# Column halves for the second batch's products with v, later scores, and dummy products only in idle steps

## Chip, cores and metric

The kernel runs on one core of a Trainium2 chip, in one launch. The metric is the device time of that core in microseconds; lower is better. Its engines are named as in the profile: PE (TensorE, with its weight loads as PEld), DVE (VectorE), ACT (ScalarE), POOL (GpSimd) and SP, which issues the DMAs.

## What is computed

Two batches of 12480 tokens of width 128. Per batch, 49 agents attend to all keys and gather v; then every query attends to the 49 agents; the result goes through a layer of width 2048 with a rational activation.

```python
def sm(a, b):
    s = scale * (a @ b.transpose(0, 2, 1))
    s = s - s.max(-1, keepdims=True)
    e = np.exp(s)
    return e / (e.sum(-1, keepdims=True) + 1e-09)
a2k = sm(agents, k)
agent_v = a2k @ v
q2a = sm(q, agents)
x = q2a @ agent_v                       # reshaped to (24960, 128)
h = x @ w_in
P = a[0] + a[1] * h + a[2] * h**2 + a[3] * h**3
Q = 1.0 + np.abs(b[0]) * np.abs(h) + np.abs(b[1]) * h**2
out = (P / (Q + 1e-06)) @ w_out
```

## The kernel before

All is float32. The first batch's attention over its keys (scores, maximum, exponentials, products with v) runs ahead of the loop, some 60 us. Its result, 49 x 128, is folded with `w_in` into a matrix of 49 rows and 2048 columns per batch (`m_pe`, L275, rounded to a high part `m_hi` and a rest `m_lo` in `m_rnd` and `m_rest`), so that the hidden layer of a block of 480 tokens is the product of this matrix with the transposed query weights `pT`.

The loop in `main` goes over 278 units of three chunks (128 hidden columns by 480 tokens). Sixteen chunks make a block of tokens; batch two begins in unit 138. Step `i` issues, each engine in its own order:

- ACT (`act`): the square of unit i (L501, out of the PSUM slot `slots[i % 2]` into `x`), and in turn the logarithm (L515) or the exponential (L517) of two earlier units.
- DVE: `dve2(i)` (L530) and `dve1(i)` (L522), which read the same slot; for one unit in four also the last product (L535).
- POOL: the last product of unit i-6 (L568) for the other three in four, and L573.
- PE: `mm1(i+1)` (L439, L440: six products into the other slot), in the first seven steps two dummy products (L578) into `outs[0]`, from step 7 on `mm2(i-7)` (L447: three products, two passes each in the trace, summed in `outs[0]` or `outs[1]`), and then one piece of attention work into the other bank of `outs`.

That piece comes from `attend`. It asks three streams in turn: `q_stream` (the queries of later blocks: scores L374, L379, L380, exponentials, transposes L401 with copies L406), `w_stream` (decoding the rest of `w_out`, L175 to L185, in the first steps), and `a2k_stream` (the second batch's attention over its keys). Each stream gives at most one item in a step. An item may hold one piece of PE work, and only one such piece goes into a step: who comes later in the list waits. What an item asks of ACT, DVE and POOL is put into `hold` and runs in the next step, behind that step's own work on the engine.

`a2k_stream` works in groups of four chunks of 128 keys (`G1 = 4`; 98 chunks are 24 groups of four and one of two): two empty items, then 25 items with scores (`sc_pe`, L222; copy by ACT, L640; maximum by DVE in `group_max`, L200 and L203), the maximum over partitions (`mx_pe1`, `mx_pe2`), 25 items with products with v (`pv_pe`, L253: each chunk's exponentials, 128 x 49, as weights, its v, 128 x 129, as the moving side, summed over the group in rows 0 to 48 of a bank; DVE adds the bank to `av_acc`, L257 and L259), the division (`av_norm`), a transpose, and four `m_pe`. In one step of ten (`K_REST`) this stream rests. All of it has to be done before unit 138.

A score group writes the bank that the group before it filled, so its first product waits until DVE's L200 has read that bank.

Of the kernel before, what the change touches and what calls it, by code (L numbers as in the profile page):

```python
# [11 lines left out]
F32 = mybir.dt.float32  # L12
# [4 lines left out]
ALU = mybir.AluOpType  # L17
# [4 lines left out]
C = 128  # L22
A = 49
DFF = 2048
NFC = DFF // 128
# [4 lines left out]
NCK = -(-N // CK)  # L30
NKP = NCK * CK
KR = 113
LO = 64
BT = 480
# [22 lines left out]
OUT_DVE = range(40, 50)  # L57

K_REST = 10
NUT, NWT, NXT = 9, 4, 2  # L60
KB, VB = 6, 6

# [8 lines left out]
WARM, DUM, DUA = 8, 2, 4  # L71
# [9 lines left out]
def agent_attention_rational_moe(  # L81
# [12 lines left out]
    PE, ACT, DVE, POOL, SP = nc.tensor, nc.scalar, nc.vector, nc.gpsimd, nc.sync  # L94

    const = ctx.enter_context(tc.tile_pool(name="const", bufs=1))
# [7 lines left out]
    ident = const.tile([128, 128], F32, name="ident")  # L104
# [12 lines left out]
    mb = const.tile([CK, 2, A], F32, name="mb")  # L117
    m49 = const.tile([A, 2], F32, name="m49")
    av_acc = const.tile([A, C + 1], F32, name="av_acc")
    avt = const.tile([128, KR], F32, name="avt")  # L120
    m_hi = [const.tile([128, DFF], F32R, name=f"m_hi{b}") for b in range(B)]
    m_lo = [const.tile([128, DFF], F32R, name=f"m_lo{b}") for b in range(B)]
# [126 lines left out]
    def pv_pe(b, G, g, bank, first, last):  # L249
        vt = v_t.pop((b, g))  # L250
        n = min(G, NCK - g * G)
        for c in range(n):
            PE.matmul(bank[:A, :C + 1], lhsT=S[:, g * G + c, :], rhs=vt[:, c, :], start=first and c == 0, stop=last and c == n - 1)  # L253

    def pv_ev(first, bank):
        if first:
            DVE.tensor_copy(out=av_acc, in_=bank[:A, :C + 1])  # L257
        else:
            DVE.tensor_tensor(out=av_acc, in0=bank[:A, :C + 1], in1=av_acc, op=ALU.add)  # L259

    def av_norm(src):
        r = ring(sm_p, 1, [A, 1], F32, "avr")
        DVE.tensor_scalar(out=r, in0=src[:, C:C + 1], scalar1=EPS, scalar2=None, op0=ALU.add)
        DVE.reciprocal(out=r, in_=r)
        DVE.tensor_scalar(out=av_acc[:, :C], in0=src[:, :C], scalar1=r, scalar2=co["rho_s"][:A], op0=ALU.mult, op1=ALU.mult)
# [150 lines left out]
    def main(wk, streams, fast):  # L416
# [54 lines left out]
        def attend(bank, blk, switching, i):  # L471
            used = switching
            for s in range(len(streams)):
                if s == 2 and i % K_REST == K_REST - 1:
                    break
                while True:
                    if nxt[s] is None:
                        nxt[s] = next(streams[s], "end")
                    if nxt[s] == "end":
                        break  # L480
                    need, pe, evs = nxt[s]
                    if need is not None:
                        if need > blk // 2 + 1:
                            break
                        nxt[s] = None
                        continue
                    if pe is not None:
                        if used:
                            break
                        used = True  # L490
                        pe(bank)
                    for e, f in evs:
                        hold[e].append(lambda f=f: f(bank))
                    nxt[s] = None
                    break

        def act(i):
            if i < NU:
# [52 lines left out]
        for i in range(NU + lag):  # L551
            act(i)
            run_hold("ACT")
            g = i - gap
            fin = [g] if 0 <= g < NU and not on_pool(g) else []
            if i == NU - 1:
                dve_last(fin.pop())
            if i < NU:
                dve2(i)
                dve1(i)  # L560
            for u in fin:
                dve_last(u)
            run_hold("DVE")
            if done is not None:
                out_ev(done)
                done = None
            if 0 <= g < NU and on_pool(g):
                POOL.tensor_tensor(out=view("u", g), in0=view("u", g), in1=view("w", g), op=ALU.mult)  # L568
            run_hold("POOL")
            a = (i, i, -1, i - 1)[i % ON_DVE]  # L570
            if 0 <= a < NU and on_pool(a):
                y = view("u", a)
                POOL.tensor_scalar(out=y, in0=y, scalar1=1.0, scalar2=arm["om"], op0=ALU.mult, op1=ALU.add)  # L573
            if i + 1 < NU:
                mm1(i + 1)
            if i < lag:
                for _ in range(DUM):
                    PE.matmul(outs[0][:, :BT], lhsT=wo[:, 0, :], rhs=wi[:, :BT], start=True, stop=True)  # L578
            cur = 0
            if i >= lag:  # L580
                done = mm2(i - lag)
                cur = units[i - lag][-1] // NFC
            if i > 0:
                attend(outs[1 - cur % 2], units[min(i + 1, NU - 1)][-1] // NFC, done is not None, i)
        if done is not None:
            out_ev(done)

# [38 lines left out]
    def a2k_stream(kv, b, G):  # L626
        ng = -(-NCK // G)
        load_k(kv, b, G, 0, 2)
        load_k(kv, b, G, 1, 2)
        yield (None, None, [])  # L630
        yield (None, None, [])
        for g in range(ng):
            if 1 <= g < ng - 1:
                load_k(kv, b, G, g + 1, 2)
            if g >= ng - 2:
                load_v(kv, b, G, g + 2 - ng, 2)

            def cp(bk, g=g):
                n = min(G, NCK - g * G)
                ACT.copy(out=S[:, g * G:g * G + n, :], in_=bk[:CK, :n * A].rearrange("p (c a) -> p c a", a=A))  # L640

            yield (None, lambda bk: sc_pe(b, G, g, bk), [("ACT", cp), ("DVE", lambda bk, g=g: group_max(G, g, bk))])
        row = 3 * ((ng - 2) // 2 % 2 == 0)
        yield (None, lambda bk: mx_pe1(bk, mx[:, row, :]), [("DVE", lambda bk: mx_ev1(bk))])
        yield (None, lambda bk: mx_pe2(bk), [("DVE", lambda bk: mx_ev2(bk))])
        for g in range(-2, ng):
            evs = []
            if g + 2 < ng:
                evs.append(("POOL", lambda bk, g=g: ex_sub(G, g + 2, POOL)))
            if 0 <= g + 1 < ng:  # L650
                evs.append(("ACT", lambda bk, g=g: ex_exp(G, g + 1)))
            if g < 0:
                yield (None, None, evs)
                continue
            if 1 <= g < ng - 1:
                load_v(kv, b, G, g + 1, 2)
            evs.append(("DVE", lambda bk, g=g: pv_ev(g == 0, bk)))
            yield (None, lambda bk: pv_pe(b, G, g, bk, True, True), evs)
        yield (None, None, [("DVE", lambda bk: av_norm(av_acc))])
        yield (None, avt_pe, [("DVE", avt_ev)])  # L660
        for pc in range(4):
            yield (None, lambda bk: m_pe(pc, bk), [("ACT", lambda bk: m_rnd(b, pc, bk)), ("DVE", lambda bk: m_rest(b, pc, bk))])
# [191 lines left out]
```

## Time and profile before

| | |
|---|---|
| median of three runs | 1321.06 us (1320.81 to 1327.85) |
| the profiled execution's own time | 1321.58 us |
| its span, first to last instruction | 1319.7 us |
| busy PE, DVE, ACT, POOL | 95%, 91%, 88%, 87% |
| mean granted PE clock | 0.992 |

Four engines are busy at once nearly all the time, so the busy shares alone name no bound. The steps are to be read stage by stage: the first steps of the loop (about 68 to 116 us), the steps with the second batch's scores (to about 313 us), those with its products with v (345 to 585 us), and the steps after 640 us, which hold only query work. PE's records overlap: a product's duration includes its way through the array, so what a product costs PE is read from one start to the next.

### The profile page before, as it was taken

How to read it: one execution, taken by the hardware profiler on the slowest of the kernel's cores; microseconds unless marked ns; L12 is line 12 of the kernel's file. 1: busy time of each engine (PE TensorE's matmuls, PEld its weight loads, DVE VectorE, ACT ScalarE, POOL GpSimd, SP SyncE). 2: the span in 40 equal slices, each digit the busy share in tenths (PEclk: the TensorE clock that was granted, in tenths of full speed). 3: DMA queues.
4: the chain of work that ended last, by engine and by line, in shares of the span. 5: the costliest groups of instructions: out<-in, count | busy, mean ns of one | idle time of the engine just before them, and what ended most of it. 6: DMA issues, size and time to landing. Idle time of an engine off the chain costs nothing.

```text
span 1319.7 us, 13309 instructions
## 1 busy us (share of the span) xinstructions
PE 1255.2 (95%) x4815; PEld 786.3 (60%) x4815; DVE 1196.1 (91%) x984; ACT 1166.5 (88%) x736; POOL 1153.7 (87%) x562
## 2 busy tenths in 40 slices
PE   8979999998999999998999999999999999999998
PEld 8756666665566566665555555655655555565553
DVE  5888999989988888988999999999999999999996
ACT  3468999998889898997999999999999999999995
POOL 3448988988999998988899999999999999999991
PEclk9989999999999999999999999999999999999999
DMA  9411111111011111100000000000000000000000
GB/s 367 184 48 47 40 55 46 40 59 38 22 57 47 41 53 48 39 27 23 16 23 30 23 15 23 23 15 23 30 23 15 23 23 31 8 30 8 16 7 26
DMA packets 22971, 56.55 MB, mean 43 GB/s; under 512 B 2800, under 2 KB 9712, under 8 KB 22896
## 3 DMA queue, kind: packets, MB, share of 16 engines
q1 hardware_dynamic: 22896, 55.61, 12.7%
q8 instruction: 40, 0.66, 0.2%
q14 instruction: 35, 0.29, 0.1%
HBM read 42.82 MB, written 12.78 MB: 42 GB/s over the span
## 4 chain that ended last, share of the span: by engine, by line
PE 47%; DVE 23%; ACT 13%; POOL 9%; issue 6%; DMA 1%; SPq 0%; DVEq 0%; POOLq 0%; ACTq 0%
PE outb L447 25%; DVE u L522 8%; DVE w L530 8%; PE slot L439 8%; PE slot L440 7%; ACT x L501 6%; POOL u L568 5%; ACT w L517 3%; POOL u L573 3%; PE outb L374 3%; ACT w L515 2%; DVE u L535 2%; PE outb L253 2%; PE bank L209 1%; PE outb L222 1%
## 5 line engine op out<-in xcount | busy, mean ns | idle before, releaser
L447 PE MATMUL outb<-u,wo 128*128 128x480 f32 x1664 | 726.2, 571 | 36.6 <-DVE pT L406 21.4
L568 POOL TENSOR_TENSOR u<-u,w 128x1440 f32<-128x1440 f32 x204 | 668.6, 3290 | 0.0
L530 DVE SCALAR_TENSOR_TENSOR w<-slot,cf,x 128x1440 f32<-128x1440 f32 x278 | 474.9, 1708 | 89.8 <-ACT x L501 85.0
L447 PEld LDWEIGHTS outb<-u,wo 128*128 128x128 f32 x1664 | 309.5, 189 | 314.3 <-issue 230.5
L501 ACT ACTIVATE x<-slot,cf 128x1440 f32<-128x1440 f32 x278 | 405.5, 1459 | 96.7 <-PE slot L440 68.4
L522 DVE SCALAR_TENSOR_TENSOR u<-x,cf,slot 128x1440 f32<-128x1440 f32 x278 | 472.6, 1700 | 0.0
L573 POOL TENSOR_SCALAR u<-u,cf 128x1440 f32<-128x1440 f32 x204 | 387.8, 1902 | 93.7 <-DVE u L522 72.5
L439 PE MATMUL slot<-pT,m_hi 113*128 113x480 f32 x832 | 375.6, 452 | 10.9 <-DVE u L522 10.5
L515 ACT ACTIVATE w<-w,cf 128x2880 f32<-128x2880 f32 (+1 forms) x140 | 374.6, 2676 | 0.0
L517 ACT ACTIVATE w<-w 128x2880 f32<-128x2880 f32 (+1 forms) x140 | 361.8, 2585 | 0.0
L440 PE MATMUL slot<-pT,m_lo 113*128 113x480 f32 x832 | 317.4, 382 | 0.0
L439 PEld LDWEIGHTS slot<-pT,m_hi 113*128 113x128 f32 x832 | 157.6, 189 | 82.8 <-DVE u L522 40.9
L440 PEld LDWEIGHTS slot<-pT,m_lo 113*128 113x128 f32 x832 | 157.9, 190 | 40.8 <-issue 23.4
L535 DVE SCALAR_TENSOR_TENSOR u<-u,cf,w 128x1440 f32<-128x1440 f32 x74 | 134.0, 1816 | 0.0
L374 PEld LDWEIGHTS outb<-ag,q 128*120 128x120 f32 x400 | 45.6, 185 | 12.7 <-issue 8.2
L374 PE MATMUL outb<-ag,q 128*120 128x49 f32 x400 | 44.9, 265 | 0.9 <-DVE pT L406 0.7
L401 PEld LDWEIGHTS outb<-ident,p 120*113 120x113 f32 x200 | 27.5, 177 | 23.2 <-issue 20.0
L222 PEld LDWEIGHTS outb<-ag,k 128*128 128x128 f32 x196 | 26.4, 197 | 15.7 <-issue 8.8
L406 DVE CAST pT<-outb 113x480 fp32r<-113x480 f32 x50 | 32.4, 648 | 0.0
L454 ACT COPY o<-outb 128x480 f32<-128x480 f32 x42 | 23.0, 547 | 9.2 <-PE outb L447 9.2
L253 PEld LDWEIGHTS outb<-v,S 128*49 128x49 f32 x196 | 20.3, 123 | 17.6 <-issue 12.0
L401 PE MATMUL outb<-ident,p 120*113 120x120 f32 x200 | 29.2, 267 | 0.0
(132 smaller groups left out, 504.3 us busy)
## 6 DMA issues: line engine op xcount, KB each, us to landing
q<-qT SPq DMA_DIRECT2D x26, 480.0 KB, 3.4
outT<-o SPq DMA_DIRECT2D x52, 240.0 KB, 2.0
v<-vP SPq DMA_DIRECT2D x24, 258.0 KB, 2.7
k<-kT SPq DMA_DIRECT2D x24, 256.0 KB, 2.6
v<-vP SPq DMA_DIRECT2D x9, 645.0 KB, 11.1
k<-kT SPq DMA_DIRECT2D x8, 640.0 KB, 8.9
raw<-w_in SPq DMA_DIRECT2D x4, 512.0 KB, 10.8
raw<-w_out SPq DMA_DIRECT2D x2, 512.0 KB, 10.6
```

The costliest lines, as they stand in the source:

```text
L374: PE.matmul(bank[:CH, c * A:(c + 1) * A], lhsT=qt[:, c * CH:(c + 1) * CH], rhs=ag[:, b * A:(b + 1) * A], start=True, stop=True)
L439: PE.matmul(s[:, j, :BT], lhsT=m_hi[b][:KR, f], rhs=rhs, start=True, stop=False)
L440: PE.matmul(s[:, j, :BT], lhsT=m_lo[b][:KR, f], rhs=rhs, start=False, stop=True)
L447: PE.matmul(outs[blk % 2][:, :BT], lhsT=wo[:, fc, :], rhs=g[:, j, :], start=fc == 0, stop=fc == NFC - 1)
L501: ACT.activation(out=x, in_=h, func=AF.Square, bias=co["xb"])
L515: ACT.activation(out=r, in_=r, func=AF.Ln, bias=arm["lb"])
L517: ACT.activation(out=r, in_=r, func=AF.Exp, scale=-1.0)
L522: DVE.scalar_tensor_tensor(out=y, in0=x, scalar=co["kap"], in1=h, op0=ALU.add, op1=ALU.mult)
L530: DVE.scalar_tensor_tensor(out=w, in0=h, scalar=co["mu"], in1=x, op0=ALU.max, op1=ALU.add)
L535: DVE.scalar_tensor_tensor(out=view("u", u), in0=view("u", u), scalar=arm["om"], in1=view("w", u), op0=ALU.add, op1=ALU.mult)
L568: POOL.tensor_tensor(out=view("u", g), in0=view("u", g), in1=view("w", g), op=ALU.mult)
L573: POOL.tensor_scalar(out=y, in0=y, scalar1=1.0, scalar2=arm["om"], op0=ALU.mult, op1=ALU.add)
```

## The change

Three edits. `K_WAIT = 6` puts six empty items ahead of the scores in place of two. The dummy products move behind `attend` and are issued only where `attend` issued no PE work in the step (`attend` now returns `used`). The products with v of the second batch (`pv2_pe`) put even chunks of a group into rows 0 to 48 of the bank and odd chunks into rows 64 to 112, each half with its own start and stop; DVE adds 113 rows instead of 49 to a new tile `av_two` (`pv2_ev`), and at the end one product with the identity brings the upper half down (`pv2_sum`) and DVE adds the halves (`pv2_both`), ahead of `av_norm` in the item that held only that.

```diff
+K_WAIT = 6
+    av_two = const.tile([KR, C + 1], F32, name="av_two")
...
+    def pv2_pe(b, G, g, bank):
+        vt = v_t.pop((b, g))
+        n = min(G, NCK - g * G)
+        for c in range(n):
+            o = c % 2 * LO
+            PE.matmul(bank[o:o + A, :C + 1], lhsT=S[:, g * G + c, :], rhs=vt[:, c, :], start=c < 2, stop=c >= n - 2)
...
+    def pv2_ev(first, bank):
         if first:
-            DVE.tensor_copy(out=av_acc, in_=bank[:A, :C + 1])
+            DVE.tensor_copy(out=av_two, in_=bank[:KR, :C + 1])
         else:
-            DVE.tensor_tensor(out=av_acc, in0=bank[:A, :C + 1], in1=av_acc, op=ALU.add)
+            DVE.tensor_tensor(out=av_two, in0=bank[:KR, :C + 1], in1=av_two, op=ALU.add)
+
+    def pv2_sum(bank):
+        PE.matmul(bank[:A, :C + 1], lhsT=ident[LO:KR, LO:KR], rhs=av_two[LO:KR, :], start=True, stop=True)
+
+    def pv2_both(bank):
+        DVE.tensor_tensor(out=av_acc, in0=bank[:A, :C + 1], in1=av_two[:A, :], op=ALU.add)
+        av_norm(av_acc)
...
-            if i < lag:
-                for _ in range(DUM):
-                    PE.matmul(outs[0][:, :BT], lhsT=wo[:, 0, :], rhs=wi[:, :BT], start=True, stop=True)
...
-            if i > 0:
-                attend(outs[1 - cur % 2], units[min(i + 1, NU - 1)][-1] // NFC, done is not None, i)
+            used = i > 0 and attend(outs[1 - cur % 2], units[min(i + 1, NU - 1)][-1] // NFC, done is not None, i)
+            if i < lag and not used:
+                for _ in range(DUM):
+                    PE.matmul(outs[0][:, :BT], lhsT=wo[:, 0, :], rhs=wi[:, :BT], start=True, stop=True)
...
-        yield (None, None, [])
-        yield (None, None, [])
+        for _ in range(K_WAIT):
+            yield (None, None, [])
...
-            evs.append(("DVE", lambda bk, g=g: pv_ev(g == 0, bk)))
-            yield (None, lambda bk: pv_pe(b, G, g, bk, True, True), evs)
-        yield (None, None, [("DVE", lambda bk: av_norm(av_acc))])
+            evs.append(("DVE", lambda bk, g=g: pv2_ev(g == 0, bk)))
+            yield (None, lambda bk: pv2_pe(b, G, g, bk), evs)
+        yield (None, pv2_sum, [("DVE", pv2_both)])
```

Counted over the order of PE's work, this moves as follows. Before, score groups stand in steps 3, 4, 5, 6 and then 10 to 51, the products with v in steps 61 to 110, the last `m_pe` in step 121. Now the first score group stands in step 10 (in steps 7 to 9 the query stream holds the place or the key stream rests), the last in 57, the products with v in 66 to 117, `pv2_sum` in 120, the last `m_pe` in step 130.

Two places in the order. First PE in steps 4 and 5, before (`k1` is a group of keys, `ag` the agents, `outb` a bank of `outs`; L439 and L440 are `mm1`, L578 the dummies, L222 a score group):

```order
L578 MATMUL outb0_67<-wi_78,wo_79 128x480 x2
L222 MATMUL outb1_68<-ag_71,k1_1_647 128x49 x4
L439 MATMUL slot0_605<-pT_0_566,m_hi0_86 128x480
L440 MATMUL slot0_605<-pT_0_566,m_lo0_88 128x480
...
L578 MATMUL outb0_67<-wi_78,wo_79 128x480 x2
L222 MATMUL outb1_68<-ag_71,k1_0_645 128x49 x4
```

and now (L457 and L458 are `mm1`, L602 the dummies):

```order
L602 MATMUL outb0_67<-wi_78,wo_79 128x480 x2
L457 MATMUL slot0_606<-pT_0_567,m_hi0_87 128x480
L458 MATMUL slot0_606<-pT_0_567,m_lo0_89 128x480
...
L602 MATMUL outb0_67<-wi_78,wo_79 128x480 x2
L457 MATMUL slot1_607<-pT_0_567,m_hi0_87 128x480
```

The scores are gone from between the dummies and the next `mm1`; in step 1 it is the dummies that are gone, ahead of the query scores.

Second DVE in steps 4 to 6, before (`w`, `u`, `x`: the loop's tiles; `qs`: the query sums, L387 and L388; `wo`: the decoded weights, L185; `mx`: the scores' maximum):

```order
L522 SCALAR_TENSOR_TENSOR u_4_632<-x_0_641,cf_74,slot0_605 128x1440
L387 TENSOR_REDUCE qs_1_755<-e1_91 120x8
L388 RECIPROCAL qs_1_755<-qs_1_755 120x8
L185 SCALAR_TENSOR_TENSOR wo_79<-u_6_634 128x512
L200 TENSOR_REDUCE mx_81<-outb1_68 128x49
L530 SCALAR_TENSOR_TENSOR w_2_639<-slot1_606,cf_74,x_1_642 128x1440
L522 SCALAR_TENSOR_TENSOR u_5_633<-x_1_642,cf_74,slot1_606 128x1440
L185 SCALAR_TENSOR_TENSOR wo_79<-w_3_640 128x512
L200 TENSOR_REDUCE mx_81<-outb1_68 128x49
L530 SCALAR_TENSOR_TENSOR w_3_640<-slot0_605,cf_74,x_0_641 128x1440
```

and now (L549 and L541 are `dve2` and `dve1`):

```order
L541 SCALAR_TENSOR_TENSOR u_4_633<-x_0_642,cf_74,slot0_606 128x1440
L405 TENSOR_REDUCE qs_1_749<-e1_92 120x8
L406 RECIPROCAL qs_1_749<-qs_1_749 120x8
L188 SCALAR_TENSOR_TENSOR wo_79<-u_6_635 128x512
L549 SCALAR_TENSOR_TENSOR w_2_640<-slot1_607,cf_74,x_1_643 128x1440
L541 SCALAR_TENSOR_TENSOR u_5_634<-x_1_643,cf_74,slot1_607 128x1440
L188 SCALAR_TENSOR_TENSOR wo_79<-w_3_641 128x512
L549 SCALAR_TENSOR_TENSOR w_3_641<-slot0_606,cf_74,x_0_642 128x1440
```

The maxima of the scores have left the first steps; nothing else changed its place there.

## Rows read from the trace of the kernel before

**Rows 1.** The page: the chain that ended last, shares of the span by engine.

```profile
PE 47%; DVE 23%; ACT 13%; POOL 9%; issue 6%; DMA 1%; SPq 0%; DVEq 0%; POOLq 0%; ACTq 0%
```

**Rows 2.** Windows: stretch, length, busy PE, PEld, DVE, ACT, POOL; clock, DMA share, GB/s.

```profile
115.99:312.73 196.74, 190.65 (x775) 124.70 (x776) 179.12 (x153) 179.66 (x120) 176.07 (x78) 1.00 0.16 48
374.67:599.56 224.89, 218.53 (x852) 134.66 (x852) 199.43 (x162) 204.66 (x132) 207.39 (x108) 1.00 0.14 42
753.38:1138.11 384.73, 368.13 (x1290) 221.36 (x1288) 362.99 (x258) 364.10 (x204) 365.79 (x161) 1.00 0.07 23
```

**Rows 3.** The same stretches, line L530 alone, which has one instruction a step.

```profile
115.99:312.73 196.74, 73.70 (x43) 1.00 0.16 48
374.67:599.56 224.89, 82.23 (x48) 1.00 0.14 42
753.38:1138.11 384.73, 153.96 (x90) 1.00 0.07 23
```

**Rows 4.** The chain of waits from 374 to 600 us: shares by line, one piece.

```profile
by line: PE outb L447 39.6%; PE slot L439 13.0%; PE slot L440 11.2%; PE outb L253 8.4%; DVE w L530 5.3%; ACT x L501 4.5%; DVE u L522 4.3%; PE outb L374 2.9%; DVE u L535 2.6%; issue 2.4%; ACT w L517 1.2%; ACT w L515 1.1%; DVE av_acc L265 1.1
...
404.15 2.42 PE outb L447 x6
```

**Rows 5.** Timeline of PE and PEld around one group of products with v (start, us).

```profile
353.34 1.77 PE L447 MATMUL outb<-u,wo 128*128 128x480 f32 x4
355.04 0.83 PEld L253 LDWEIGHTS outb<-v,S 128*49 128x49 f32 x8 [0.70 <-issue]
355.05 1.09 PE L253 MATMUL outb<-v,S 128*49 128x129 f32 x8
356.06 0.48 PE L439 MATMUL slot<-pT,m_hi 113*128 113x480 f32 x1
356.39 0.38 PE L440 MATMUL slot<-pT,m_lo 113*128 113x480 f32 x1
356.60 0.38 PE L439 MATMUL slot<-pT,m_hi 113*128 113x480 f32 x1
```

**Rows 6.** Groups by line: these products' durations (min/median/max ns), and two copies by DVE.

```profile
L253 PE MATMUL outb<-v,S x196: 271/273/313, 355.0 to 584.1; 128*49 128x129 f32 x196
...
L238 DVE COPY mb<-outb 128x49 f32<-128x49 f32 x3 | 0.6, 204 | 0.9 <-PE outb L235 0.9
...
L257 DVE COPY av_acc<-outb 49x129 f32<-49x129 f32 x1 | 0.3, 278 | 0.0
```

**Rows 7.** Timeline of PE in steps 3 to 5, two score groups among them.

```profile
82.36 0.99 PE L222 MATMUL outb<-ag,k 128*128 128x49 f32 x8
84.53 0.49 PE L439 MATMUL slot<-pT,m_hi 113*128 113x480 f32 x1 [1.19 <-DVE u L522]
...
85.95 1.77 PE L578 MATMUL outb<-wi,wo 128*128 128x480 f32 x4
91.42 1.88 PE L222 MATMUL outb<-ag,k 128*128 128x49 f32 x8 [3.70 <-DVE mx L200]
93.09 0.75 PE L439 MATMUL slot<-pT,m_hi 113*128 113x480 f32 x1
```

**Rows 8.** Window behind PE's idle stretch (columns as Rows 2).

```profile
91.50:98.30 6.80, 6.80 (x18) 4.99 (x19) 4.86 (x5) 2.87 (x4) 5.62 (x6) 0.50 0.14 39
```

**Rows 9.** Waits from 86 to 120 us (total us, times, longest).

```profile
DVE w L530 <- ACT x L501: 3.6, 3, 1.9
```

**Rows 10.** Timeline of DVE and POOL from step 4 to step 10.

```profile
87.88 1.70 DVE L522 SCALAR_TENSOR_TENSOR u<-x,cf,slot 128x1440 f32<-128x1440 f32 x1
...
97.42 3.29 POOL L568 TENSOR_TENSOR u<-u,w 128x1440 f32<-128x1440 f32 x1
...
110.18 1.46 POOL L573 TENSOR_SCALAR u<-u,cf 128x1440 f32<-128x1440 f32 x1
114.06 2.79 POOL L573 TENSOR_SCALAR u<-u,cf 128x1440 f32<-128x1440 f32 x1 [2.42 <-DVE u L522]
116.82 3.28 POOL L568 TENSOR_TENSOR u<-u,w 128x1440 f32<-128x1440 f32 x1
```

More of the change, by code (lines that the diff above doesn't have):

```diff
@@ L253, in pv_pe @@
             PE.matmul(bank[:A, :C + 1], lhsT=S[:, g * G + c, :], rhs=vt[:, c, :], start=first and c == 0, stop=last and c == n - 1)
-    def pv_ev(first, bank):
+    def pv2_pe(b, G, g, bank):
[5 more added lines that the diff above has]
+    def pv2_ev(first, bank):
         if first:
-            DVE.tensor_copy(out=av_acc, in_=bank[:A, :C + 1])
+            DVE.tensor_copy(out=av_two, in_=bank[:KR, :C + 1])
         else:
-            DVE.tensor_tensor(out=av_acc, in0=bank[:A, :C + 1], in1=av_acc, op=ALU.add)
+            DVE.tensor_tensor(out=av_two, in0=bank[:KR, :C + 1], in1=av_two, op=ALU.add)
[4 more added lines that the diff above has]
+        av_norm(av_acc)
     def av_norm(src):
@@ L495, in attend @@
                     break
+            return used
         def act(i):
```

## The prediction

> **What bounds the kernel now.** The chain that ended last runs 47% through PE, 23% through DVE, 13% through ACT [rows 1]: no engine holds the whole time, so I went from the page to windows over stages. Three stretches with an even mix of steps, each cut at the start of a step, give the busy time of every engine [rows 2], and the same stretches with L530 alone give the number of steps [rows 3]. A step takes 196.74 / 43 = 4.575 us while the second batch's scores run, 224.89 / 48 = 4.685 us while its products with v run, and 384.73 / 90 = 4.275 us with neither. PE is busy 97% of the first two stretches and the others 89 to 92% [rows 2]; in the products' stretch the chain is 75% PE (L447, L439, L440, L253, L374) [rows 4]. So PE leads there, with the others close behind.
>
> From this come two prices on the path. The first stretch holds 21 score groups (counted in the order), each with ACT's copy and DVE's maximum: (4.575 - 4.275) x 43 / 21 = 0.61 us a group. The second holds 22 groups of products with v: (4.685 - 4.275) x 48 / 22 = 0.89 us. PE's own time for one of these is more: a pass of `mm2` takes 2.42 / 6 = 0.40 [rows 4], so the four from 353.34 would end their turn at 354.94; the group starts at 355.05, L439 at 356.06, and L440 comes 0.33 later, where the next pass takes 0.21 or 0.22. That is 0.11 + 1.01 + 0.11 = 1.23 us [rows 5]. So 0.89 / 1.23 = 0.73 of PE's time shows in the end.
>
> The loop's first steps are another matter. DVE paces them; but in step 4 PE's queue stops for 3.70 us at a score group that needs the bank which L200 has yet to read, until 91.42 [rows 7]. Behind it stands `mm1(6)`, whose slot was free when L522 of step 4 ended at 89.58 [rows 10]. It starts at 93.09, at half clock: PE did nothing for those 3.70 us, and the granted clock is 0.50 (1.2 GHz) from 91.5 to 98.3 [rows 8]. DVE then waits three times for ACT's squares, 3.6 us in all [rows 9].
>
> **The change, part by part.** *Scores out of steps 3 to 6.* PE's queue then holds only `mm1` and dummies, and `mm1(6)` can start at about 89.6, 3.5 us earlier. DVE's 3.6 us of waits go, and four maxima with them. What is late next is POOL. Its first L568, at 97.42, hangs on decoded weights that DVE delivers hardly sooner, and from there POOL is almost without a gap until it waits 2.42 us for step 9's L522 [rows 10]. With DVE ahead this wait goes: POOL's next L568 moves up from 116.82 by 2.4 us, by 0.3 more from L200's absence, and by up to 1.3 more if the L573 at 114.06 takes the 1.46 us of the one at 110.18 instead of 2.79 [rows 10]. That makes 2.7 to 4.0; I take **3.4 us** gained at step 10. Below this there may be nothing, if PE's clock falls anyway (a rival).
>
> *Dummies out of step 1.* Two products, four passes of 0.40 us. PE waits for DVE there, so the gain is nothing; what it costs if the clock falls belongs to the same rival.
>
> *The four score groups come back later.* Steps 10 to 52 hold the same kinds of work as before, and everything behind is later by some nine steps, into steps 122 to 130, which had no key work. The deadline, step 137, is met. Four groups at 0.61 us (copies and maxima included) cost **2.5 us**. The k and v loads are issued with these items and move along; the loop's DMAs use 16% of the engines [rows 2], so I cost that at nothing, and a load that came late would stop PE itself.
>
> *`pv2_sum`.* One product of two passes, one addition on DVE. It has two passes of the eight of a group and both ends of one: between 0.2 and 0.9 us, taken as **0.4**, since the ends (0.22) stay whole.
>
> *DVE's addition over 113 rows instead of 49.* The same 129 elements a row. A copy out of PSUM of 128 rows by 49 takes 204 ns and one of 49 rows by 129 takes 278 [rows 6]: time goes with the elements in a row, not with the rows, so I take nothing. Were it in proportion to the rows, 25 additions would take 25 x 0.28 x 64 / 49 = 9 us more of a DVE that is 89% busy; the 128-row copy excludes that.
>
> *Column halves.* Eight passes start over 1.09 - 0.27 = 0.82 us, the first with 0.04 extra for its load (313 against 273 ns): 0.78 / 7 = 0.111 us a pass, the load of the next hidden under the pass before (eight loads within 0.83 us) [rows 5, 6]. If two halves of the array work at once, the order of the passes limits it: both passes of a chunk go to one half and follow each other, so only the second pass of a chunk can overlap the first of the next, in three places per group. That is 3 x 0.111 = 0.33 us if the other half's load is hidden too, 3 x 0.07 = 0.21 if its 0.04 is not. I take 0.27. No row shows two halves at work, so the ends are nothing below and 4 x 0.111 = 0.44 above (all passes paired), and a loss if a switch costs something. As to how much reaches the end: 0.73 on average, all of it while PE leads; I take 0.85. 24 groups x 0.27 x 0.85 = **5.5 us**.
>
> Sum: -3.4 + 2.5 + 0.4 - 5.5 = -6.0 us. The profiled execution took 1321.58 us, 1.9 of it outside the span, and the median of the runs is 1321.06, 0.5 below. From the median: **1315.1 us**, 0.45% faster. About 0.5%, 6.6 us, is what a measurement of this kernel can tell from no change, so the forecast lies at that edge.
>
> **Rivals.** *The halves don't overlap.* The column position is set but passes still go one by one at 0.111 us. For: every load and pass in the trace is in order. Against: a load already goes under a running pass [rows 5]. Then -3.4 + 2.9 = -0.5: 1320.6 us. The Trainium skill (TensorE: Matmul & The Clock Gate, Part 3: Packing small matmuls) says that a weight load overlaps running products only where their row groups differ; both halves here use all 128 rows, so by that rule this is how it goes. The trace disagrees so far, with eight loads inside 0.83 us, under the passes of the same rows. The same section measures 2.38 times the rate for three column tiles, which would be the next rival.
>
> *The halves overlap fully*, by pairs: 24 x 0.44 x 0.85 = 9.0 saved in place of 5.5, 1311.6 us. Against: the order of the passes.
>
> *Each change of half drains the array.* Entering a group costs 0.11 us, and leaving it holds L440 by another 0.11 [rows 5]: some 0.2 for one out and one in. Three changes in a group: 24 x 0.6 x 0.85 = 12.2, no overlap, 1332.8 us. It is slower by over 0.5% from 0.12 us a change on. The Trainium skill (TensorEngine Tiling (Array Packing), Key Properties) says that a change of mode drains TensorE and a change of tile alone does not; no run here shows a change of tile.
>
> *PE goes cold in the first steps.* Without the dummies of step 1 PE runs ahead, and without the score of step 3 it idles from about 81.4 (82.36 before, where that score starts) to 84.5, when DVE frees the slot [rows 7]: 3.1 us, near the 3.70 after which the clock fell [rows 7, 8]. Half a clock doubles `mm1` and dummies from 2.9 to 5.8 us, more than a step of DVE. If that lasts to step 7, the 3.4 us are lost: 1318.5 us. Against: DVE's steps 4 and 5 leave room for most of it.
>
> **How the numbers follow.** Forecast 0.50, no overlap 0.13, full overlap 0.18, drain 0.07, cold start 0.12. The forecast's own range is 1312 to 1317.5 (0.33 us a group at 1.0 and the start at 4.0; 0.21 at 0.73 and 2.7); some 0.22 of its 0.50 lies beyond 0.5%. Faster: 0.22 + 0.18 = 0.40; same: 0.28 + 0.13 + 0.12 = 0.53; slower: 0.07. The range takes in no overlap above, and below full overlap with all of it reaching the end (24 x 0.44 = 10.6, so 1310.0) and the start at its upper end: 1308.5 to 1321.5.
>
> **What would show it.** The profile after should have `mm1(6)` start before 91 us, no wait of L222 for L200 there, and granted clock 1.00 from 85 to 100; step 10's L530 near 112 instead of 116. The products with v should start in pairs, a group going from 0.82 to about 0.55 us between its first and last pass, and a step of that stage should last about 4.57 us instead of 4.685. If the passes keep 0.111, the halves did nothing; if a group grows, they drain. A last `m_pe` that stops unit 138 would make all of it wrong.

## The result and the profile after

The changed kernel takes **1308.92 us** in the median of four runs (1306.39 to 1317.1), the kernel before 1324.45 beside it (1320.81 to 1328.04): ratio 0.9879, interval 0.9838 to 0.9921. That is 1.2% faster; the forecast was 0.45%, so the sign was right and the size was not. Two of the four runs before (1327.85 and 1328.04) and one of the four after (1317.1) are some 8 us longer than the rest, so the median before lies between the two kinds; the shorter runs alone have medians of 1320.94 and 1308.21 us, 12.7 us or 1.0% apart. The two profiled executions, 1321.58 and 1306.39 us, lack the stall that the longer profiled ones show in the last steps (further down), and are compared here.

The page after, busy times and chain by engine (for the second see [rows 1]):

```profile
PE 1240.9 (95%) x4813; PEld 773.2 (59%) x4813; DVE 1194.4 (92%) x985; ACT 1166.5 (89%) x736; POOL 1154.5 (88%) x562
...
PE 45%; DVE 23%; ACT 14%; POOL 10%; issue 7%; DMA 0%; POOLq 0%; DVEq 0%; SPq 0%; ACTq 0%
```

Nothing in these two lines tells where 15 us went; the stages do. Windows after over the same steps as [rows 2] (10 to 52, 66 to 113, 149 to 238; same columns):

```profile
109.73:306.89 197.16, 191.56 (x781) 125.20 (x780) 178.97 (x153) 180.53 (x120) 178.06 (x79) 1.00 0.16 49
366.19:584.30 218.11, 208.91 (x853) 124.32 (x851) 198.54 (x159) 203.15 (x132) 209.12 (x110) 1.00 0.16 46
738.42:1123.12 384.70, 367.75 (x1290) 221.23 (x1288) 363.07 (x258) 364.20 (x204) 365.91 (x161) 1.00 0.07 23
```

The scores' stretch is as long as before (197.16 for 196.74 us) and so is the one with queries alone; the products' stretch fell from 224.89 to 218.11, with PE's busy time down from 218.53 to 208.91. The rest must lie between. Steps are counted by `dve2`, one instruction a step (L530 before, L549 after), and "the loop" in this document runs from its first start to that of the last: 1229.96 us before, 1217.17 after, **12.78 less**. Of the other 2.4 us of the 15.2, 2.28 lie ahead of the loop, in code that the change leaves alone; there the profiled executions of all kernels differ between 66.1 and 71.6 us. So 12.78 is what has to be explained, not 15.5 between the medians. By steps, in us against before:

| steps | 0-9 | 10-52 | 53-65 | 66-109 | 110-122 | 123-130 | 131-276 | loop |
|---|---|---|---|---|---|---|---|---|
| after | -3.99 | +0.42 | -2.63 | -5.29 | -3.25 | +2.51 | -0.55 | -12.78 |

The forecast knew three of these: the start, the products and the moved work in 123 to 130. Of the 5.9 us in steps 53 to 65 and 110 to 122 it knew little. Each such row here and below is one execution: in steps 131 to 276, which the edits leave alone, executions without the stall differ by up to 1.1 us, so a single entry under 1 us proves nothing.

**The start came as forecast.** PE in step 4 and the clock in the first steps; then DVE in step 10 and POOL ahead of it:

```profile
87.36 0.49 PE L457 MATMUL slot<-pT,m_hi 113*128 113x480 f32 x1 [1.93 <-DVE u L541]
```

```profile
88.40:91.80 3.40, 3.40 (x7) 1.56 (x5) 3.40 (x3) 3.40 (x3) 2.86 (x3) 0.50 0.00 0
85.00:100.00 15.00, 11.72 (x33) 6.23 (x32) 14.84 (x13) 14.92 (x9) 13.28 (x12) 0.89 0.00 0
```

```profile
107.67 4.36 POOL L592 TENSOR_SCALAR u<-u,cf 128x1440 f32<-128x1440 f32 x2
109.73 1.71 DVE L549 SCALAR_TENSOR_TENSOR w<-slot,cf,x 128x1440 f32<-128x1440 f32 x1
111.99 6.54 POOL L587 TENSOR_TENSOR u<-u,w 128x1440 f32<-128x1440 f32 x2
```

`mm1(6)` starts at 87.36, which with the 2.28 us added is 89.64 on the scale of before (forecast 89.6; 93.09 before [rows 7]); step 10 starts at 109.73, or 112.01 (forecast 112; 116.0 before). POOL's wait of 2.42 us [rows 10] is gone. The sign on the clock failed: PE idles 1.93 us and then runs at half clock (0.50, 1.2 GHz) from 88.4 to 91.8, so 0.89 over 85 to 100. It was at 0.50 from 71.3 to 78.1 too, behind an idle stretch of 2.05 us. No cost of either shows: step 10 comes when it was forecast.

**The groups run in pairs.** PE around one group after (compare [rows 5]):

```profile
367.81 1.77 PE L465 MATMUL outb<-u,wo 128*128 128x480 f32 x4
369.51 0.65 PE L264 MATMUL outb<-v,S 128*49 128x129 f32 x8
370.09 0.48 PE L457 MATMUL slot<-pT,m_hi 113*128 113x480 f32 x1
```

```profile
369.51 0.39 PEld L264 LDWEIGHTS outb<-v,S 128*49 128x49 f32 x8 [0.70 <-ACT o L472]
```

Eight passes take 0.65 us in place of 1.09, their loads 0.39 in place of 0.83: four pairs with starts 0.11 to 0.15 us apart (the two of a pair differ by 6 to 8 ns). The trace doesn't record which half a pass uses; that the two of a pair stand in different halves is inferred from the edit, since without it no two passes start together. The forecast had 0.27 of this 0.44. The Trainium skill (TensorEngine Tiling (Array Packing), Key Properties) says that different tiles load and multiply in parallel and that a change of tile alone does not drain; these rows agree. The sentence of the Trainium skill (TensorE: Matmul & The Clock Gate, Part 3: Packing small matmuls) that a load overlaps running products only where row groups differ does not hold here: both halves use all 128 rows.

**What the forecast did not see.** In the kernel before, DVE and POOL around the diagonal of the maxima (L232, step 54) and the last scaling (L265, step 112); the windows of PE behind each:

```profile
319.01 6.54 POOL L568 TENSOR_TENSOR u<-u,w 128x1440 f32<-128x1440 f32 x2
...
322.26 3.33 DVE L232 TENSOR_SCALAR d<-ident,m 49x49 f32<-49x49 f32 x1
...
328.89 0.49 PE L439 MATMUL slot<-pT,m_hi 113*128 113x480 f32 x1 [1.92 <-DVE u L522]
...
590.82 3.30 POOL L568 TENSOR_TENSOR u<-u,w 128x1440 f32<-128x1440 f32 x1
...
591.52 0.15 DVE L264 RECIPROCAL avr<-avr 49x1 f32<-49x1 f32 x1
591.72 2.48 DVE L265 TENSOR_SCALAR av_acc<-av_acc,avr,cf 49x128 f32<-49x128 f32 x1
...
599.70 1.60 PE L447 MATMUL outb<-u,wo 128*128 128x480 f32 x2 [3.65 <-DVE pT L406]
```

```profile
330.50:333.90 3.40, 3.40 (x5) 1.35 (x5) 3.40 (x4) 3.39 (x2) 1.48 (x2) 0.50 0.00 0
600.10:603.50 3.40, 3.40 (x9) 2.35 (x8) 2.79 (x2) 0.00 (x0) 3.40 (x2) 0.50 0.04 15
```

An operation on 49 rows of 49 elements takes 3.33 us, and ends at 325.59, when the second of POOL's pair of products ends (325.55). That product alone:

```profile
322.25 3.31 POOL L568 TENSOR_TENSOR u<-u,w 128x1440 f32<-128x1440 f32 x1
```

It had started 0.02 us ahead of DVE's operation, which then stood for all of it. The second small operation ends at 594.20, POOL's product at 594.12. While they stand, DVE's work of the next unit stands behind them, PE waits for that work (idle 1.92 us for a slot, 3.65 us for the bank that DVE's copy L406 reads), and the clock falls to 0.50 after each. After the change the same two operations fall elsewhere between POOL's:

```profile
349.00 6.51 POOL L587 TENSOR_TENSOR u<-u,w 128x1440 f32<-128x1440 f32 x2
...
351.17 1.15 DVE L235 TENSOR_SCALAR d<-ident,m 49x49 f32<-49x49 f32 x1
...
618.92 2.79 POOL L592 TENSOR_SCALAR u<-u,cf 128x1440 f32<-128x1440 f32 x1 [0.15 <-DVE u L541]
...
620.97 0.81 DVE L283 TENSOR_SCALAR av_acc<-av_acc,avr,cf 49x128 f32<-49x128 f32 x1
```

They take 1.15 and 0.81 us, and in this execution the clock stays at 1.00 from 115 to 1290 us. In all executions in which DVE still does them, both small operations end 0.04 to 0.08 us after the end of an instruction of POOL; how long they stand depends on when in that instruction they start. The Trainium skill (SBUF — State Buffer, Who interferes with whom) says that a scaling of this kind from SBUF to SBUF can take the pair of ports that DVE shares with GpSimd, for the whole instruction, and that the later of the two blocks; the ends at 325.59 and 325.55 agree.

The clock that stays up behind the last scaling is in part luck. PE waits 2.17 us for this scaling also after the change; the same wait in the kernel with another order of passes (a run told of below), and the windows behind each:

```profile
621.84 0.26 PE L286 MATMUL outb<-ident,av_acc 49*128 49x49 f32 x1 [2.17 <-DVE av_acc L283]
...
621.90:625.30 3.40, 3.40 (x12) 2.25 (x13) 3.40 (x4) 1.85 (x3) 3.40 (x2) 1.00 0.00 0
```

```profile
623.73 0.26 PE L287 MATMUL outb<-ident,av_acc 49*128 49x49 f32 x1 [2.16 <-DVE av_acc L284]
...
625.00:628.30 3.30, 3.30 (x7) 1.76 (x6) 2.94 (x4) 2.40 (x2) 3.30 (x2) 0.50 0.00 0
```

In six kernels profiled with the change's places for the two operations (the change and the five that follow from it below with both on DVE), the scaling takes 0.81 us; behind it the clock stays at 1.00 in three and falls to 0.50 in three. Two of the latter allow a price: their steps 110 to 130 are 1.6 and 1.7 us longer than the change's.

### The profile page after: what moved, and what is told of

It is laid out like the page before. It is cut to its first block, busy times and chain, and to the rows that moved or that the text cites. A ratio compares the mean times of both kernels' runs of the same rounds, so it can differ in the third digit from the quotient of the medians.

```text
span 1304.6 us, 13303 instructions
## 1 busy us (share of the span) xinstructions
PE 1240.9 (95%) x4813; PEld 773.2 (59%) x4813; DVE 1194.4 (92%) x985; ACT 1166.5 (89%) x736; POOL 1154.5 (88%) x562
## 3 DMA queue, kind: packets, MB, share of 16 engines
q1 hardware_dynamic: 22896, 55.61, 12.8%
HBM read 42.82 MB, written 12.78 MB: 43 GB/s over the span
## 4 chain that ended last, share of the span: by engine, by line
PE 45%; DVE 23%; ACT 14%; POOL 10%; issue 7%; DMA 0%; POOLq 0%; DVEq 0%; SPq 0%; ACTq 0%
PE outb L465 24%; DVE u L541 9%; DVE w L549 8%; PE slot L457 7%; ACT x L520 7%; PE slot L458 7%; POOL u L587 6%; ACT w L536 3%; POOL u L592 3%; PE outb L392 3%; ACT w L534 3%; DVE u L554 2%; PE bank L212 1%; PE outb L225 1%; DVE pT L424 1%
## 5 line engine op out<-in xcount | busy, mean ns | idle before, releaser
L465 PE MATMUL outb<-u,wo 128*128 128x480 f32 x1664 | 724.4, 569 | 37.1 <-DVE pT L424 19.5
L549 DVE SCALAR_TENSOR_TENSOR w<-slot,cf,x 128x1440 f32<-128x1440 f32 x278 | 475.2, 1709 | 78.7 <-ACT x L520 73.2
L465 PEld LDWEIGHTS outb<-u,wo 128*128 128x128 f32 x1664 | 308.4, 189 | 314.5 <-issue 229.5
L541 DVE SCALAR_TENSOR_TENSOR u<-x,cf,slot 128x1440 f32<-128x1440 f32 x278 | 472.8, 1701 | 0.0
L457 PE MATMUL slot<-pT,m_hi 113*128 113x480 f32 x832 | 373.9, 449 | 11.1 <-DVE u L541 10.6
L458 PE MATMUL slot<-pT,m_lo 113*128 113x480 f32 x832 | 316.5, 380 | 0.0
L457 PEld LDWEIGHTS slot<-pT,m_hi 113*128 113x128 f32 x832 | 157.0, 189 | 84.5 <-DVE u L541 43.0
L458 PEld LDWEIGHTS slot<-pT,m_lo 113*128 113x128 f32 x832 | 157.5, 189 | 39.9 <-issue 22.7
L392 PEld LDWEIGHTS outb<-ag,q 128*120 128x120 f32 x400 | 46.8, 189 | 12.3 <-issue 8.2
L392 PE MATMUL outb<-ag,q 128*120 128x49 f32 x400 | 46.0, 269 | 0.8 <-DVE av_two L270 0.6
L419 PEld LDWEIGHTS outb<-ident,p 120*113 120x113 f32 x200 | 27.5, 177 | 25.2 <-issue 22.5
L419 PE MATMUL outb<-ident,p 120*113 120x120 f32 x200 | 29.1, 267 | 1.9 <-DVE av_two L270 1.9
L184 POOL TENSOR_TENSOR r<-r,s 128x512 f32<-128x512 f32 x6 | 9.2, 1534 | 22.8 <-DVE s L181 22.8
```

The costliest lines, as they stand in the source:

```text
L392: PE.matmul(bank[:CH, c * A:(c + 1) * A], lhsT=qt[:, c * CH:(c + 1) * CH], rhs=ag[:, b * A:(b + 1) * A], start=True, stop=True)
L457: PE.matmul(s[:, j, :BT], lhsT=m_hi[b][:KR, f], rhs=rhs, start=True, stop=False)
L458: PE.matmul(s[:, j, :BT], lhsT=m_lo[b][:KR, f], rhs=rhs, start=False, stop=True)
L465: PE.matmul(outs[blk % 2][:, :BT], lhsT=wo[:, fc, :], rhs=g[:, j, :], start=fc == 0, stop=fc == NFC - 1)
L541: DVE.scalar_tensor_tensor(out=y, in0=x, scalar=co["kap"], in1=h, op0=ALU.add, op1=ALU.mult)
L549: DVE.scalar_tensor_tensor(out=w, in0=h, scalar=co["mu"], in1=x, op0=ALU.max, op1=ALU.add)
```

## The experiments

My theory after these profiles: the stalls of the two small operations (the time for which they hold up DVE, and PE behind it) explain the missing five microseconds, the rest is the forecast's terms. Rivals: the halves are worth more than I said (they overlap fully); or the dummies' edit keeps the clock up. Ratios are against the kernel before, run beside each.

**Each edit alone.** First the column halves, with `K_WAIT` and the dummies as before:

```diff
-K_WAIT = 6
+K_WAIT = 2
+            if i < lag:
+                for _ in range(DUM):
...
-            if i < lag and not used:
-                for _ in range(DUM):
```

> Measured by the loop, from the first L530 (step 0) to the last (step 277): 1229.95 us before, 1217.17 after the whole change. Theory A (several parts: faster start, cheaper products, two stalls that the new places avoid): the halves alone give the products' part only, 25 groups with the passes paired (0.38 us from first to last pass instead of 0.82) and some 0.6 to 0.8 of the 0.44 us reaching the end, so a loop of 1221 to 1224 us, the start unchanged (step 10 at +47.6 us) and the stalls around steps 54 and 115 as before. Theory B (the halves are all of it, at full price and with PE's stalls gone because PE has slack): 1217 to 1220 us.

Then the kernel before with the other two edits, with `K_WAIT = 6` alone, and with the dummies' edit alone:

> Both other edits without the halves. Theory A: 4.0 us gained by step 10, 2.5 lost by four score groups later, and 4 to 6 us gained where the maximum (steps 53 to 60) and the division (steps 113 to 120) no longer meet a long POOL instruction: a loop of 1222 to 1225 us. Theory B: only the start's 4.0 less 2.5, so 1228 to 1229 us.

> Six empty items alone, dummies in all of the first seven steps. Both theories: the start's gain comes from the scores that left, so step 10 comes 43.6 us after step 0 as in the whole change (47.6 before), and the loop is that of the run with both edits within 1 us. If the dummies' edit carries the start, step 10 stays at 47 us or more.

> The dummies' edit alone: they go from steps 1, 3, 4, 5 and 6, where attention work stands, scores stay there. Theory A: PE is not what paces these steps, so nothing to 1 us gained by step 10 and the stop of the second score group for the maximum stays; PE may be colder, up to 3 us lost. Rival: a dummy in front of the score holds PE up, 1 to 3 us gained.

Measured: halves 0.9944 (0.9917 to 0.9971); both others 0.9972 (0.9949 to 0.9995); later scores alone 0.9964 (0.9939 to 0.999); dummies alone 1.0015 (0.9988 to 1.0042). By steps, us against before:

| steps | 0-9 | 10-52 | 53-65 | 66-109 | 110-122 | 123-130 | 131-276 |
|---|---|---|---|---|---|---|---|
| halves | -0.43 | +0.03 | -0.91 | -4.92 | -3.96 | +0.91 | +0.32 |
| both others | -4.01 | +0.35 | -2.57 | -0.82 | +0.15 | +2.54 | +6.92 |
| later scores | -4.03 | +0.46 | -2.64 | -0.70 | +0.10 | +2.51 | +6.85 |
| dummies alone | +2.47 | +0.08 | -0.57 | +0.08 | +0.97 | 0.00 | +7.08 |

The start's 4.0 us belong to the later scores; the dummies' edit alone loses 2.5 there, with the clock at 0.50 from 84.1 to 107.9 us and PE's waits for the maxima up from 3.7 to 5.5: the cold start that I had as a rival is real, where the scores stay. The 2.5 us forecast for the four score groups appear in steps 123 to 130, where the key stream now ends. But each kernel also moves the two small operations. With the halves alone L235 still takes 3.34 us in step 54 (cold 328.1 to 331.5) and the last scaling only 0.90; with later scores alone L232 takes 1.14 and the last scaling 3.42, now in step 119 (cold 630.7 to 634.1). So the 3.96 us in steps 110 to 122 of the first are no gain of the halves' passes, and these four runs alone don't add up to the parts. Their expectations missed by this: the first two took both stalls as there or both as gone, and each kernel has one of them (loops 1220.99 and 1232.52 us, the second with 6.9 of the stall in the last steps). (The 7 us in the last steps of three of them are the stall told of at the end.)

**The two small operations off DVE.** The diagonal and the last scaling go to ACT, each in an item of its own; DVE keeps only the 49 x 1 ones:

```diff
-        DVE.tensor_scalar(out=st["d"], in0=ident[:A, :A], scalar1=m49[:, k:k + 1], scalar2=None, op0=ALU.mult)
+        ACT.activation(out=st["d"], in_=ident[:A, :A], func=AF.Copy, scale=m49[:, k:k + 1])
...
-        DVE.tensor_scalar(out=av_acc[:, :C], in0=src[:, :C], scalar1=r, scalar2=co["rho_s"][:A], op0=ALU.mult, op1=ALU.mult)
+            DVE.tensor_scalar(out=r, in0=r, scalar1=co["rho_s"][:A], scalar2=None, op0=ALU.mult)
...
+        ACT.activation(out=av_acc[:, :C], in_=av_acc[:, :C], func=AF.Copy, scale=st["r"])
```

On the kernel before, and on the change:

> The kernel before, with two small products (the diagonal of maxima, L232, and the last scaling of the division, L265) moved from DVE to ACT, each in an item of its own, so the key stream is two steps longer. In the profile before they take 3.33 and 2.48 us on DVE, ending when a POOL instruction ends, and PE goes cold behind each (330 to 334 and 600 to 603 us). Theory A (these two, held up by POOL, cost the time that the change regained by moving them): neither cold window is left, the loop is 3 to 5 us shorter than 1229.96, so 1225 to 1227 us, with the last product of step 273 at about 3.1 us on DVE; where it takes 9.5 us, 6 to 8 us more. Theory B (the cold windows come from the order of the steps, not from these two): 1229 us or more.

> The same edit on the changed kernel, where the two take 1.15 and 0.81 us and no cold window follows. Theory A: 0 to 1.5 us gained, a loop of 1215.7 to 1217.2 us. Theory B: no tie between the two edits; as much as it gains or loses on the kernel before.

and later, to price the halves where neither side has such a stall, on the halves alone:

> Column halves alone, with both small products (diagonal of the maxima, last scaling) on ACT. Beside the run of the kernel before with the same two products on ACT (loop 1224.65 us) only the halves and their sum differ, with no small operation of DVE that waits for POOL in either. Theory (the halves are worth 0.20 to 0.24 us a group, half of the 0.44 by which a group's passes got shorter, less a little for the sum): loop 1219 to 1220 us, and the clock not at half anywhere between 110 and 1290 us. Rival (0.85 of 0.44 us reaches the end, and the 66 to 110 steps hide part of it by chance): loop 1215.5 to 1217 us. Second rival (the halves are worth what I wrote, 5.5 us, only because the wait at the last scaling went): loop 1222 to 1224 us.

Measured: 0.9965 (0.9938 to 0.9992), 0.9914 (0.9884 to 0.9943), 0.9918 (0.9889 to 0.9946); loops 1224.65, 1216.94 and 1217.76 us. (The ratios are gains of 4.6, 11.4 and 10.8 us; the loops, of one execution each, give 5.3, 13.0 and 12.2.) Without the stalls the clock is 1.00 from 115 us on in the kernel before too (window of that kernel):

```profile
115.00:1290.00 1175.00, 1131.57 (x4146) 692.12 (x4145) 1087.85 (x823) 1093.33 (x651) 1097.62 (x495) 1.00 0.10 30
```

The loop gains 5.31 us on the kernel before and 0.23 on the change: the theory holds. Read as a path, before to after, the four differences add up to the whole by the way they are made; the last two rows are of the size by which unchanged stretches differ:

| from | to | us | of it |
|---|---|---|---|
| before | both small operations on ACT | -5.31 | the two stalls |
| that | with the halves and their sum | -6.89 | -1.22 in the first steps, -5.67 behind |
| that | with later scores and dummies | -0.82 | -2.53 in the first steps, +1.71 behind |
| that | the change | +0.23 | small operations back on DVE |

The 1.22 in the first steps comes with no edit there: PE was at half clock from 93.5 to 96.9 us in that execution, from 92.3 to 99.1 in the other. The start's share of the change is thus 2.5 to 4.0 us, by how long the clock of before is down.

The halves give 5.67 us in 24 groups, 0.24 each; I had expected a loop of 1219 to 1220 and it is 1217.76, by those first steps. Why 0.24, when a group's passes got 0.44 shorter? Groups by line of PE with both small operations on ACT, from within step 61, just ahead of the first group, to the end of step 122: first without the halves, then with them (line, operation, shape, count | busy us, mean ns | idle before, by what ended it):

```profile
L459 PE MATMUL outb<-u,wo 128*128 128x480 f32 x370 | 161.1, 567 | 4.9 <-DVE pT L418 4.0 <-DVE av_acc L264 0.9
...
L258 PE MATMUL outb<-v,S 128*49 128x129 f32 x196 | 26.8, 278 | 0.0
L386 PE MATMUL outb<-ag,q 128*120 128x49 f32 x96 | 10.9, 266 | 0.2 <-DVE av_acc L264 0.2
```

```profile
L477 PE MATMUL outb<-u,wo 128*128 128x480 f32 x367 | 159.9, 568 | 6.9 <-DVE pT L436 4.0 <-DVE av_two L275 2.8
...
L269 PE MATMUL outb<-v,S 128*49 128x129 f32 x196 | 16.0, 283 | 0.0
L404 PE MATMUL outb<-ag,q 128*120 128x49 f32 x96 | 10.9, 266 | 0.9 <-DVE av_two L275 0.9
L431 PE MATMUL outb<-ident,p 120*113 120x120 f32 x40 | 5.9, 268 | 1.6 <-DVE av_two L275 1.6
```

The products' busy time falls by 10.8 us (26.8 to 16.0), and PE's waits for DVE's addition of the group rise from 1.1 to 5.3: 4.2 of it come back as a **new wait**. The bank that a group fills is wanted by the next PE work, and DVE adds it behind its two large operations, no earlier than before. Steps 61 to 122 got 7.0 us shorter and 123 to 130 1.7 longer, because two of the four `m_pe` now fall there: 5.3 net. Against it stand 10.8 - 4.2 = 6.6 less 0.4 for `pv2_sum`'s two passes; some 0.9 us stays unexplained.

**Does the order of passes matter?** Chunks 0, 1 below and 2, 3 above, in place of alternating:

```diff
-            o = c % 2 * LO
+            h = n // 2
+            o = c // h * LO
```

> The changed kernel with the first two chunks of a group in the lower half and the last two in the upper, so the products come in the order lower, lower, upper, upper instead of in turn. If PE only lets neighbours in different halves run together, one place of three is left where halves meet: the group's eight passes start over 0.60 to 0.71 us instead of 0.38, and the loop is 3 to 5 us longer. If it looks further ahead than the neighbour, 0.38 us stay and the loop stays at 1217.2 within 1 us.

One group of this kernel:

```profile
371.44 0.66 PE L265 MATMUL outb<-v,S 128*49 128x129 f32 x8
```

0.66 against 0.65 us: the order within a group doesn't matter, and the step of the forecast that counted meeting places (0.27 us) falls. One run took 1309.86 us. Its loop is 1218.96 us, 1.8 more than the change's and not within 1 us as expected; 1.7 of it lie in steps 110 to 130, with the fall of the clock shown above.

**Twice the products**, each group's passes issued two times (the sum of these products is doubled):

```diff
-        for c in range(n):
+        for c in [*range(n), *range(n)]:
             o = c % 2 * LO
```

> The changed kernel with each group's products with v issued twice (the second set begins its sums anew, so the result is that of the changed kernel): eight more passes, some 0.44 us more PE time in each of 25 groups, about what the halves took away, with nothing else moved. If half of PE's time there reaches the end, the loop is 5.5 us longer, 1222 to 1224; if 0.85 as the prediction took, 9 us, 1226 to 1227; if PE has slack there, under 2 us.

One run, 1325.09 us, loop 1231.68, of which 7.5 are the stall of the last steps: 7.0 us more than the change for 25 x 0.44 = 11 us of passes. Here too the clock falls behind the last scaling, from 631.5 us on; at the 1.6 us that this costs above, 5.4 are left for the passes, about half (an estimate). PE's L465 from 366 to 640 us:

```profile
L465 PE MATMUL outb<-u,wo 128*128 128x480 f32 x352 | 153.7, 569 | 5.0 <-DVE pT L424 3.7 <-DVE av_two L270 0.6 <-POOL u L587 0.5
...
L264 PE MATMUL outb<-v,S 128*49 128x129 f32 x392 | 26.8, 277 | 0.0
```

As long as before, the passes leave no wait for the addition (0.6 us; in the change it is 4.6 with L392 and L419). So passes made longer and passes made shorter show much the same trade.

**The addition earlier**, between DVE's two large operations:

```diff
-        hold = {"ACT": [], "DVE": [], "POOL": []}
+        hold = {"ACT": [], "DVE0": [], "DVE": [], "POOL": []}
...
                 dve2(i)
+                run_hold("DVE0")
                 dve1(i)
...
-            evs.append(("DVE", lambda bk, g=g: pv2_ev(g == 0, bk)))
+            evs.append(("DVE0", lambda bk, g=g: pv2_ev(g == 0, bk)))
```

> The change, with DVE's addition of a group of products with v (L268, L270) between its two large operations of the step (L549 and L541) in place of behind both. In the change PE waits 4.6 us for L270 from 366 to 625 us (in the kernel before 0.9 us for L259 from 375 to 600): the groups end 0.44 us earlier, but the bank that they fill comes free when DVE has added it, and DVE gets there no earlier. Theory (these waits are what the halves give back): PE's waits for this addition fall under 1.5 us, steps 66 to 123 get 2.5 to 4 us shorter, loop 1213 to 1215 us where the change has 1217.17. Rival (the wait only moves: L541 is 0.28 us later in 24 steps, and PE waits for it instead): loop 1216.5 to 1218 us, with waits of PE for L541 in place of those for L270. Second rival (DVE now stands at the addition until PE has finished the group, and the next unit is late): loop over 1219 us.

Measured: 0.9924 (0.9897 to 0.9951), 1308.4 to 1318.15 us. PE's L465 from 366 to 630 us:

```profile
L465 PE MATMUL outb<-u,wo 128*128 128x480 f32 x352 | 152.8, 568 | 8.5 <-POOL u L588 4.7 <-DVE pT L424 3.8
```

The wait for the addition is gone, and 4.7 us of waits for POOL's products (0.6 in the change) are in its place: the next engine was close behind. Steps 66 to 122 get 1.6 us shorter than in the change, not 2.5 to 4, nor nothing; both expectations missed. Its profiled loop, 1223.15, holds 7.4 us of the stall in the last steps.

**The last steps.** In the profiled executions with a long end, as here with later scores alone, DVE's last product of unit 267 (step 273) starts in the second of four products of POOL that follow each other without a gap:

```profile
1281.07 9.47 DVE L535 SCALAR_TENSOR_TENSOR u<-u,cf,w 128x1440 f32<-128x1440 f32 x1
```

```profile
1276.09 12.93 POOL L568 TENSOR_TENSOR u<-u,w 128x1440 f32<-128x1440 f32 x4
```

POOL is through at 1289.02, and DVE only then gets its 1.5 us. In the change's execution it started in the second as well and got in behind it (3.06 us, and POOL's four took 14.40). Two kernels took that meeting away from the change:

```diff
-        return u % ON_DVE != ON_DVE - 1 and u < NU - LAST_DVE
+        return (u % ON_DVE != ON_DVE - 1 or u == NU - 11) and u < NU - LAST_DVE
...
-            if 0 <= a < NU and on_pool(a):
+            for a in (a, i) if i == NU - 11 else (a,):
+                if not (0 <= a < NU and on_pool(a)):
+                    continue
```

> The change, and unit 267's last product with its addition on POOL in place of DVE's L554, so that DVE has no two-operand product beside POOL's four L587 in a row. Theory (the 9.46 us of that L554 in some executions is DVE kept out by POOL's products that follow each other without a gap, and the 7 to 8 us longer runs are those executions): no run of this kernel is 7 us above the others, the median is 1306 to 1309 us, and the loop is within 2 us of the 1217.17 of the change. Rival (the longer runs have another cause): some runs at 1314 to 1318 us all the same, as with the change (1317.1). Second rival: POOL gets late by the 4 us of one more unit, and the end of all runs is 2 to 4 us later, 1310 to 1313 us.

```diff
-ON_DVE, LAST_DVE = 4, 7
+ON_DVE, LAST_DVE = 4, 11
```

> The change, and the last eleven units' last products on DVE in place of the last seven (LAST_DVE = 11): POOL has no work left beside L554 of the last steps. Theory (as for the kernel before it): no long L554 and no run 7 us above the others; DVE has three more products of 1.63 us, 4.9 us, of which part shows: 1307 to 1312 us. Rival (another cause of the longer runs): some runs at 1314 to 1319 us.

Measured: 0.9898 (0.986 to 0.9935), five runs from 1308.81 to 1312.91 and one at 1319.07; and 0.9962 (0.9936 to 0.9988), median 1319.2, its last 77 steps 5.2 us longer than the change's, about its three more products of 1.63 us. The first has its loop at 1216.68 and no long product in the profile, but one long run; the second spreads from 1313.51 to 1325.95 us. Both missed the expectation that no run would be long. So this product is where the time goes in every profile with a long end, and not the only way to it; what makes a long run where the meeting is gone stays open, since none of those was profiled. No experiment can be told from the change as faster.

## Why the prediction was right and wrong

- *What bounds the kernel*: right as far as the stages show. A products' step takes 218.11 / 48 = 4.544 us, forecast 4.57.
- *Start, -3.4*: -4.0 in the profiles, at its upper bound, with every time on the way as forecast; but in three executions without the later scores the first steps were 0.3, 0.4 and 1.5 us shorter too. The clock did fall, for 6.8 and 3.4 us, at no cost that shows.
- *Four score groups, +2.5*: **the step that failed.** It priced what the moved work adds where it arrives (measured +1.71, with the dummies' edit and without stalls), and took everything behind it to cost the same some nine steps later, without a term for that. But two small operations of DVE had taken 3.33 and 2.48 us, waiting for POOL, and PE had gone cold behind them; at their new places they take 1.15 and 0.81. They start 2.17 and 2.05 us into an instruction of POOL there, in place of 0.02 and 0.90; nobody chose these places, so that is luck, and so is the clock behind the second. It is 5.1 us of gain which the sum has no term for (5.31 with both on ACT, less the 0.23 still left). I had read the chain with L265 in it at 1.1% of the products' stretch [rows 4], 2.5 us for 49 x 128 elements, and did not ask why.
- *`pv2_sum` and halves, +0.4 - 5.5 = -5.1*: measured -5.67 together. Right in sum by two errors: the passes got shorter by 0.44, not 0.27 (the order doesn't limit them), and some 0.55 of it reached the end, not 0.85. That share was taken from a stretch in which PE was the later side; a saving on PE alone ends where the next one, here DVE's addition, is due.
- *Addition over 113 rows at nothing*: its duration, yes: 0.28 us (L270, 6.8 us for 24). Its place in DVE's queue became the wait.
- *Rivals*: no overlap and a draining change of half are refuted by the 0.65 us a group. Full overlap was the true one in form; its price of 9.0 us was too high, by the new wait for the most part. The cold start happens with the dummies' edit alone.
- *Range*: its lower end, 1308.5, was said to be full overlap with all of it reaching the end and the start at 4.0; these terms give 1309.4.

Sum of the terms as measured: -5.1 - 5.67 - 3.75 + 1.71 = -12.8 us, with -3.75 for the two shares in the first steps, and the loop's -12.78. The forecast's -6.0 lacks the first term and little else.

## To carry to other kernels

Before you move work in a kernel with full queues, look for operations that take far longer than their elements explain, and for the instruction of another engine that ends when they do; moving anything may dissolve or create such a meeting, and that can outweigh the edit itself. A saving on one engine reaches the end up to the next engine's due time: follow the buffer that comes free and ask who frees it. Where parts don't add up one by one, remove the chance meeting from all sides first and measure then.

## What was not expected of the hardware

- A DVE scaling of 49 x 49 elements took 3.33 us: it started 0.02 us after a POOL product and ended 0.04 us after that product's end. A product of DVE with both operands in SBUF took 9.47 us, through the rest of one POOL product and two whole ones; in other executions of nearly the same steps it got in after the first (3.06 us).
- Behind the same wait of PE (2.16 to 2.17 us for the last scaling) the granted clock fell to 0.50 in some executions and stayed at 1.00 in others.
- PE overlapped the passes of two column halves in pairs, four pairs in 0.39 us of loads, also where neighbours in the order went to the same half (0.66 against 0.65 us for the group).
